# Transposes of 32-bit tiles moved from TensorE to the DMA queue, as two planes of 16 bits

## The chip, the cores and the metric

The kernel runs on one core of a Trainium2 chip. The core has TensorE (PE; PEld is its weight load), VectorE (DVE), ScalarE (ACT), GpSimd (POOL), SyncE (SP), which here only issues DMAs, and 16 DMA engines. The time of a run is device microseconds (us) from start to end; lower is better. A profiled execution has its own time, and inside it a span, which the trace covers.

## What is computed

```python
def reference(A_x, A_wqkv, A_wo, B_x, B_w1, B_w2):     # B_x is not used
    xn = layernorm(A_x)                                  # [1, 2048, 640], eps 1e-5
    q, k, v = split(xn @ A_wqkv)                         # 32 heads of 20
    # each position attends to 8 positions: itself, 2, 4, ... 14 before it
    s = softmax_attention(q, k, v, scale=20 ** -0.5) @ A_wo
    g = silu(silu(xn @ B_w1) @ B_w2)                     # 640 -> 1536 -> 640
    return A_x + s * g
```

All tensors are 32-bit floats. The kernel keeps their precision by splitting both sides of a product into a high part (the number as a float32r) and a low part, the rest. A product is then three matmuls: high x high, low x high, high x low.

## The kernel before

**Tiles and stages.** The 2048 rows are worked on in four groups of 512, that is four token tiles of 128 (T = 4). A group holds every second position of one half of the sequence (`groups`, L193), four of them on each partition, so that positions 2 apart are neighbours. For each group there are two stages. `qkv_phase` (L731) multiplies the transposed input by wqkv in four quarters of the heads (NQ = 4, eight heads each): five units of the inner dimension (DC = 5) for four token tiles, three matmuls each, into four of six PSUM banks (acc). `ffn_phase` (L945) runs the feed-forward: twelve hidden chunks of 128 (FC = 12), each an `up` (L895, 15 matmuls into one of two PSUM banks, rot) and a `down` (L922, 24 matmuls into acc). Its order is a list from `plan` (L288): w1 0, then pairs of two up and two down. `wo_phase` (L798) of the group before, the output projection, stands after w1 0. The last group's projection is `wo_last` (L842), after everything else.

**Attention on DVE.** `evac_qkv` (L526) copies a quarter from PSUM to Q and KV on ACT, `halo` (L539) shifts KV by one and two partitions by four DMAs on SP's queue (L548), `scores` (L565) and `values` (L588) do the attention on DVE with operations of 2560 elements, an exp on ACT between them (L586) from L into E. The result is O, one tile for all of a group's 640 columns. DVE works on a group while TensorE is in its feed-forward stage and in the next group's qkv stage.

**Transposes.** A matmul needs its 128 inner elements on the partitions, so the normalized input (XIN) and O must be turned. The first group's input is turned on TensorE in `first_quarter` (L669). All others go through `split_t` (L503): four transposes of 128x128 on TensorE (L509) into one rot bank, a copy of the high part on ACT (L513) to TH, and the low part on DVE (L519, L516) to TL. One call turns one chunk, 128 of the 640 columns for all four token tiles. The input's five chunks stand between the pairs of the feed-forward stage of the group before, with a second copy on ACT (L515) that frees the rot bank. O's five chunks (`o_chunk`, L615) stand in the next group's qkv stage, after the last units of quarters 1, 2 and 3 (`O_AT`, L769). In the last group three chunks of O stand between single up and down units (`OL_AT`, L192; `SINGLE`, L32), and the last two chunks are turned by halves of the token tiles (`o_rest`, L619), the second half inside the last up. OH and OL, where O's halves go, are the same memory as TH and TL, 16 elements on.

**The order.** The functions only record operations. `Weave` (L65) then places them in time with a cost for each, and the program is written out in that order. TensorE's order is that of recording. On the other engines the earliest ready operation goes first, by priority among those (a priority of 140 or more gives way to others that are ready soon, L136). DMAs on SP have an issue cost, a rate (`RATE`, L75) and a landing time. Each engine then runs its instructions strictly in the written order, and waits where an input is not there. SP's queue carries raw weights, stores of the split weights, loads of x, the halo shifts and the output; POOL's queue the loads of split weights, which each later use reads back from memory. Weights lie in a ring of seven buffers (WR).

Of the kernel before, what the change touches and what calls it, by code (L numbers as in the profile page):

```python
# [8 lines left out]
F32 = mybir.dt.float32  # L9
F32R = mybir.dt.float32r  # L10
AF = mybir.ActivationFunctionType
# [20 lines left out]
SINGLE = 6  # L32
# [32 lines left out]
class Weave:  # L65
# [9 lines left out]
    RATE = 310e3  # L75
# [104 lines left out]
def local_attention_silu_ffn(ctx: ExitStack, tc: tile.TileContext, x, wqkv, wo, w1, w2, out):  # L180
# [11 lines left out]
    OL_AT = {8: 0, 9: 1, 10: 2}  # L192
# [95 lines left out]
    def plan(g):  # L288

        last = g == NG - 1
        todo = [("w1", 0)] + [("wo", 0)] * (g > 0)
        down = 0
        f = 1
        while f < FC:
            k = f // 2
            pair = f + 1 < FC and not (last and f > SINGLE)
            if not last and 1 <= k <= DC:
                todo.append(("x", k - 1))  # L300
            if last and f in OL_AT:
                todo.append(("o", OL_AT[f]))
            if last and f == FC - 1:
                todo.append(("rest", (0, 1)))
# [198 lines left out]
    def split_t(src, skeys, c, i, to, whole=None):  # L503

        ps, kp = rot()

        def turn():
            for t in range(T):
                nc.tensor.transpose(ps[:, tsl(t)], src[:, t, c * P:(c + 1) * P], ident)  # L509
        pe(0.44, turn, skeys, [kp])  # L510
        hi, lo = to[0][i][:, c, :], to[1][i][:, c, :]
        kh, kl = t_keys(i, [c], kinds=["th"]), t_keys(i, [c], kinds=["tl"])
        act(TOK, lambda: nc.scalar.activation(hi, ps, AF.Copy), [kp], kh, 0)  # L513
        if whole is not None:
            act(TOK, lambda: nc.scalar.activation(whole, ps.rearrange("p (t n) -> p t n", n=P), AF.Copy), [kp] + skeys, [("whole", c)], 0)  # L515
            dve(TOK, lambda: nc.vector.tensor_tensor(out=lo.rearrange("p (t n) -> p t n", n=P), in0=whole,  # L516
                in1=hi.bitcast(F32).rearrange("p (t n) -> p t n", n=P), op=OP.subtract), kh + skeys + [("whole", c)], kl, 0, lock=True)
            return
        dve(TOK, lambda: nc.vector.tensor_tensor(out=lo, in0=ps, in1=hi.bitcast(F32), op=OP.subtract),  # L519
            [kp] + kh, kl, 0)  # L520
# [44 lines left out]
    def scores(g, q):  # L565
        i = q % 2
        l, e, m, kv, qq = L[i], E[i], M[i], KV[q], Q[q]
# [18 lines left out]
        act(256, lambda: nc.scalar.activation(e, l, AF.Exp, scale=SCALE), kl, [("e", i)], 0.5, "exp")  # L586

    def values(g, q):  # L588
        i = q % 2
        e, z, kv = E[i], Z[i], KV[q]  # L590
# [3 lines left out]
            out=z[:, 0], in_=e.rearrange("p t w h -> p t h w"), axis=AX.X, op=OP.add), [("e", i)], [("z", i)], pr)  # L594
        dve(200, lambda: nc.vector.reciprocal(out=z[:, 1], in_=z[:, 0]), [], [("z", i)], pr)
        dve(256, lambda: nc.vector.tensor_tensor(out=e, in0=e, in1=win(z[:, 1], W, 0), op=OP.mult),
            [("z", i)], [("e", i)], pr, lock=True)
        for t in range(0, T, 2):
# [7 lines left out]
                in1=v, op=OP.mult), [("e", i)] + hk, PRK, pr, lock=True)  # L606
# [7 lines left out]

    def o_chunk(g, c, i):  # L615
        qs = range(c * P // CQ, ((c + 1) * P - 1) // CQ + 1)
        split_t(O, [("o", q, t) for q in qs for t in (0, 2)], c, i, (OH, OL))

    def o_rest(g, ts, i):  # L619

        ps, kp = rot()
        cs = slice(DC - 2, DC)
        v = ps.rearrange("p (c n) -> p c n", c=2)
        hi, lo = (o[i][:, cs, ts[0] * P:(ts[-1] + 1) * P] for o in (OH, OL))

        def turn():
            for k, c in enumerate(range(DC)[cs]):
                for n, t in enumerate(ts):
                    nc.tensor.transpose(v[:, k, tsl(n)], O[:, t, c * P:(c + 1) * P], ident)  # L629
        pe(0.44, turn, [("o", q, ts[0]) for q in (NQ - 2, NQ - 1)], [kp])  # L630
        kh, kl = (t_keys(i, range(DC)[cs], ts, [k]) for k in ("th", "tl"))
        act(TOK, lambda: nc.scalar.activation(hi, v, AF.Copy), [kp], kh, 0)
        dve(TOK, lambda: nc.vector.tensor_tensor(out=lo, in0=v, in1=hi.bitcast(F32), op=OP.subtract), [kp] + kh, kl, 0)
# [134 lines left out]

    O_AT = {(1, 4): (0, 1), (2, 4): (2, 3), (3, 4): (4,)}  # L769
# [23 lines left out]
    def gkeys(ts, cs):  # L793
        return [("g", t, cs.start) for t in range(ts.start, ts.stop)]
# [47 lines left out]
    def wo_last(g, i):  # L842
# [13 lines left out]
        def give(p, kp, t, cs):  # L856
            n = cs.stop - cs.start
            dve(n, lambda: nc.vector.tensor_tensor(out=G[:, t, cs], in0=p, in1=G[:, t, cs], op=OP.mult),  # L858
                [kp], [("g", t, cs.start)], 0)
            dve(n, lambda: nc.vector.tensor_tensor(out=xr[t][:, cs], in0=xr[t][:, cs], in1=G[:, t, cs], op=OP.add),  # L860
                [("g", t, cs.start)], kx(t, cs)[1:], 0, lock=True)
# [33 lines left out]
    def up(g, i, f, io):  # L895
# [11 lines left out]
        at = 2 if g == NG - 1 and f == FC - 1 else DC  # L907
        for a, b in ((0, at), (at, DC)):
            if a == b:
                continue  # L910
            if a:
                o_rest(g, (2, 3), io)
                wo_rest(g - 1, io)
            pe(3 * (b - a) * mm(TOK), lambda a=a, b=b: first(range(a, b)), t_keys(i, range(DC)) + [kh, kl], [kp])
# [29 lines left out]

    def ffn_phase(g, i, ix, io):  # L945
        if g + 1 < NG:
            load_x(g + 1, 0, 2)
            load_x(g + 1, 2, 2)
            for t in range(T):
                ln_stats(t)  # L950
            ln_rstd(0, T)
            for t in range(T):
                ln_apply(t)
        ps = None
        for kind, f in plan(g):
            if kind == "w1":
                up(g, i, f, io)
            elif kind == "wo":
                wo_phase(g - 1, io)
            elif kind == "x":  # L960
                split_t(XIN, [("xin", t) for t in range(T)], f, ix, (TH, TL), XIN[:, :, tsl(f)])
            elif kind == "o":
                o_chunk(g, f, io)
            elif kind == "rest":
                o_rest(g, f, io)
            else:
                ps = ps or tm_banks()
                down(f, ps)
        for p, kp, ts, cs in tm_views(ps):
            n = (ts.stop - ts.start) * (cs.stop - cs.start)  # L970
            act(n, lambda p=p, ts=ts, cs=cs: nc.scalar.activation(G[:, ts, cs], p, AF.Silu), [kp], gkeys(ts, cs), 0, "silu")
# [40 lines left out]
```

## Time and profile before

| | |
|---|---|
| Median of 3 runs | 636.61 us (636.52 to 636.62) |
| The profiled execution | 636.8 us |
| Its span | 635.0 us |
| TensorE busy | 629.7 us, 99% |
| DVE, ACT, POOL busy | 538.1, 220.6, 112.9 us |
| DMA | 160.82 MB, mean 253 GB/s |

Busy time counts what an engine executes, without waits and without issuing DMAs. A group of the trace is one line of the kernel, engine and operation, with output, inputs, shape and count, then its busy time, the mean of one in ns, and the idle time of the engine before it with what ended it. A matmul's duration is a latency: several are in flight at once. The chain of waits follows the work that ended last back from the end, and its pieces don't overlap.

### The profile page before, as it was taken

The page shows a single profiled execution, that of the slowest core. Times are in us where ns is not written, and L with a number is a line of the kernel's source. Part 1 is how long each engine was busy: PE and PEld are TensorE (multiplying, and loading weights), DVE is VectorE, ACT ScalarE, POOL GpSimd, SP SyncE. Part 2 cuts the span into 40 slices and gives each one's busy share as a digit, 9 for nine tenths or more (in the row PEclk, how much of TensorE's full clock was granted, in tenths as well). Part 3 has the DMA queues.
Part 4 walks back from the last instruction along what each step waited for, and adds up shares of the span by engine and source line. Part 5 has one row for each costly group of instructions (what it writes and reads, how often), then busy time and mean ns, then how long its engine had stood idle before and what let it go on. Part 6 is the DMA issues. An engine that isn't in the chain of part 4 may idle for free.

```text
span 635.0 us, 9113 instructions
## 1 busy us (share of the span) xinstructions
PE 629.7 (99%) x3503; PEld 570.1 (90%) x3503; DVE 538.1 (85%) x548; ACT 220.6 (35%) x459; POOL 112.9 (18%) x159
## 2 busy tenths in 40 slices
PE   9999999999999999999999999999999999999997
PEld 7888899998889999999888999999988999999997
DVE  6599899999999969998969998999605999999734
ACT  5436455443436024242423512323313232223230
POOL 4500000001110161111221115311222211111100
PEclk9999999999999999999999999999999999999999
DMA  9999999768997997567798998856779998666552
GB/s 294 310 304 318 319 395 375 311 220 245 297 311 221 283 292 247 175 191 211 204 255 208 310 361 305 287 176 183 220 197 268 247 324 251 182 191 195 189 177 83
DMA packets 77500, 160.82 MB, mean 253 GB/s; under 512 B 9248, under 2 KB 38912, under 8 KB 77456
## 3 DMA queue, kind: packets, MB, share of 16 engines
q0 software_dynamic: 25952, 79.31, 42.7%
q1 hardware_dynamic: 50960, 80.52, 39.7%
q8 instruction: 27, 0.44, 0.3%
q10 hardware_dynamic: 544, 0.41, 0.2%
q14 instruction: 17, 0.14, 0.1%
HBM read 107.91 MB, written 34.16 MB: 224 GB/s over the span
## 4 chain that ended last, share of the span: by engine, by line
PE 99%; DVE 0%; POOL 0%; issue 0%; POOLq 0%
PE acc L780 22%; PE acc L782 15%; PE acc L748 10%; PE acc L749 10%; PE acc L747 10%; PE rot L904 9%; PE rot L906 9%; PE rot L905 9%; PE rot L509 2%; PE acc L690 2%; PE rot L642 1%; PE rot L669 0%; PE rot L890 0%; PE rot L629 0%; DVE gate L858 0%; DVE xin L860 0%
## 5 line engine op out<-in xcount | busy, mean ns | idle before, releaser
L571 DVE TENSOR_TENSOR pr<-q,kv 128x2560 f32<-128x2560 f32 x32 | 90.3, 2820 | 34.0 <-DMA kv<-kv 33.8
L747 PE MATMUL acc<-w,th 128*128 128x512 f32 (+2 forms) x300 | 113.3, 378 | 0.0
L780 PE MATMUL acc<-w,sh 128*128 128x384 f32 x384 | 113.2, 334 | 0.0
L749 PE MATMUL acc<-w,th 128*128 128x512 f32 (+2 forms) x300 | 112.9, 376 | 0.0
L748 PE MATMUL acc<-w,tl 128*128 128x512 f32 (+2 forms) x300 | 112.9, 376 | 0.0
L782 PE MATMUL acc<-w,sh 128*128 128x256 f32 x384 | 107.1, 279 | 0.0
L904 PE MATMUL rot<-th,w 128*128 128x512 f32 x240 | 95.8, 399 | 0.0
L906 PE MATMUL rot<-th,w 128*128 128x512 f32 x240 | 93.8, 391 | 0.0
L905 PE MATMUL rot<-tl,w 128*128 128x512 f32 x240 | 93.6, 390 | 0.0
L603 DVE TENSOR_TENSOR pr<-e,kv 128x2560 f32<-128x2560 f32 x32 | 90.3, 2823 | 0.7
L574 DVE TENSOR_REDUCE l<-pr 128x128 f32<-128x2560 f32 x32 | 90.1, 2815 | 0.4
L437 POOL DMA_DIRECT2D w<-half_q x52 | 37.4, 719 | 237.8 <-PE rot L906 115.1
L437 POOL DMA_DIRECT2D w<-half_w x72 | 38.6, 536 | 215.6 <-PE acc L782 87.5
L608 DVE TENSOR_TENSOR pr<-pr 128x1280 f32<-128x1280 f32 x64 | 73.8, 1153 | 1.0
L782 PEld LDWEIGHTS acc<-w,sh 128*128 128x128 f32 x384 | 72.2, 188 | 1.0
L780 PEld LDWEIGHTS acc<-w,sh 128*128 128x128 f32 x384 | 72.1, 188 | 1.0
L917 ACT ACTIVATE sh<-rot 128x512 fp32r<-128x512 f32 x48 | 28.8, 600 | 125.4 <-PE rot L906 125.4
L749 PEld LDWEIGHTS acc<-w,th 128*128 128x128 f32 x300 | 56.3, 188 | 8.7
L748 PEld LDWEIGHTS acc<-w,tl 128*128 128x128 f32 x300 | 56.3, 188 | 8.6
L747 PEld LDWEIGHTS acc<-w,th 128*128 128x128 f32 x300 | 56.3, 188 | 8.5
L780 PE MATMUL acc<-w,sl 128*128 128x384 f32 x192 | 57.8, 332 | 0.0
L906 PEld LDWEIGHTS rot<-th,w 128*128 128x128 f32 x240 | 45.0, 188 | 9.9
(96 smaller groups left out, 993.1 us busy)
## 6 DMA issues: line engine op xcount, KB each, us to landing
w<-half_w POOLq DMA_DIRECT2D x72, 640.0 KB, 4.9
w<-half_q POOLq DMA_DIRECT2D x39, 512.0 KB, 4.6
half_w<-w SPq DMA_DIRECT2D x24, 640.0 KB
kv<-kv SPq DMA_DIRECT2D x16, 560.0 KB
kv<-kv SPq DMA_DIRECT2D x16, 420.0 KB
w<-half_wo POOLq DMA_DIRECT2D x10, 640.0 KB, 5.3
gate<-in_B_w_dram SPq DMA_DIRECT2D x16, 320.0 KB
w<-half_q POOLq DMA_DIRECT2D x13, 384.0 KB, 5.0
```

The lines of the kernel that those rows point to most:

```text
L437: add("POOL", 1.0, lambda: nc.gpsimd.dma_start(both, src), [("half", u), ("half", u, "more")], [kh, kl], due + 10, nbytes=2 * n * P * 4)
L571: dve(2560, lambda t=t: nc.vector.tensor_tensor(out=PR, in0=win(qq[:, t:t + 2, :], W, 0), in1=win(kv[:, 0, t:t + 2, :], W, CQ), op=OP.mult ...
L574: dve(2560, lambda t=t: nc.vector.tensor_reduce(out=l[:, t:t + 2].rearrange("p t w h -> p (t w h)"), in_=PR.rearrange("p t w (h d) -> p (t ...
L603: dve(2560, lambda t=t, v=v: nc.vector.tensor_tensor(out=PR.rearrange("p t w (h d) -> p t (w h) d", d=DH), in0=e[:, t:t + 2].rearrange("p ...
L747: nc.tensor.matmul(o, hi, wh, start=c == 0, stop=False)
L748: nc.tensor.matmul(o, lo, wh, start=False, stop=False)
L749: nc.tensor.matmul(o, hi, wl, start=False, stop=c == DC - 1)
L780: nc.tensor.matmul(a[t][0][:, :CA], st, w[:, :CA], start=first, stop=last)
L782: nc.tensor.matmul(b[t // 2][0][:, h * CB:(h + 1) * CB], st, w[:, CA:], start=first and h == 0, stop=last, skip_group_check=True)
L904: nc.tensor.matmul(h, wh[:, cs], TH[i][:, c, :], start=c == 0, stop=False)
L905: nc.tensor.matmul(h, wh[:, cs], TL[i][:, c, :], start=False, stop=False)
L906: nc.tensor.matmul(h, wl[:, cs], TH[i][:, c, :], start=False, stop=c == DC - 1)
```

## The change

`split_t`, `o_chunk` and `o_rest` go, and with them every transpose on TensorE past the first group's input. In their place stand `turn_chunk`, `turn_o` and `turn_rest`. A new scratch tile, `TURN`, has 512 words of 32 bits for each partition. For one chunk, ACT copies the chunk as 1024 16-bit numbers into TURN, the low halves of all words ahead of the high halves (two planes). Two DMA transposes on SP's queue, one for each plane, write the planes back, turned, in the chunk's own place in XIN or O. ACT copies them into TURN again, as words. From TURN, ACT makes the high part and DVE the low part. All chunks use the one tile, so one chunk follows the other.

- The input's chunks are recorded right behind wo in the feed-forward stage (behind w1 0 in the first group), and O's chunks at the end of that stage; both have priority 150. In the last group three chunks of O and two passes of `turn_rest` follow wo.
- `plan` has pairs throughout, also in the last group, and wo stands after the first pair (after w1 0, 1, 2) and no longer after w1 0. The last up is no longer cut in two.
- To make room for TURN, E becomes the last 64 of the 160 columns of each token tile of Q, of the same quarter, and the last group's gate lies in KV[0] (`GL`).
- The planner's `RATE` goes from 310e3 to 380e3.

```diff
-    RATE = 310e3
+    RATE = 380e3
...
-    E = tiles("e", 2, [P, T, W, HQ])
+    E = [v[:, :, CQ - W * HQ:].rearrange("p t (w h) -> p t w h", w=W) for v in Q]
...
+    GL = KV[0].rearrange("p s t m -> p (s t m)")[:, :T * D].rearrange("p (t d) -> p t d", t=T)
...
+    TURN = sb.tile([P, TOK], F32, name="turn")
...
-        todo = [("w1", 0)] + [("wo", 0)] * (g > 0)
+        todo = [("w1", 0)]
...
-            pair = f + 1 < FC and not (last and f > SINGLE)
+            pair = f + 1 < FC
...
+            if f == 1 and g:
+                todo.append(("wo", 0))
...
+    def halves_of(v, hi, lo, kh, kl):
+        act(TOK, lambda: nc.scalar.activation(hi, v, AF.Copy), ["turn"], kh, 0)
+        dve(TOK, lambda: nc.vector.tensor_tensor(out=lo, in0=v, in1=hi.bitcast(F32), op=OP.subtract),
+            ["turn"] + kh, kl, 0, lock=True)
...
+    def turn_chunk(src, keys, c, i, to, prio):
+
+        place = src[:, :, c * P:(c + 1) * P].bitcast(U16)
+        flat = place.rearrange("p t (h n) -> p h t n", h=2)
+        planes = TURN.bitcast(U16).rearrange("p (h n) -> p h n", h=2)
+        act(2 * TOK, lambda: nc.scalar.activation(
+            planes.rearrange("p h (t n) -> p h t n", t=T), place.rearrange("p t (n h) -> p h t n", h=2), AF.Copy),
+            keys, ["turn"], prio)
+        for h in range(2):
+            dma(lambda h=h: nc.sync.dma_start_transpose(flat[:, h], planes[:, h]), ["turn"], [("plane", h)],
+                P * TOK * 4, clock[0], 0.65)
+        act(2 * TOK, lambda: nc.scalar.activation(
+            TURN.bitcast(U16).rearrange("p (t n h) -> p h t n", t=T, h=2), flat, AF.Copy),
+            [("plane", 0), ("plane", 1)] + keys, ["turn"], prio)
+        halves_of(TURN, to[0][i][:, c, :], to[1][i][:, c, :], t_keys(i, [c], kinds=["th"]), t_keys(i, [c], kinds=["tl"]))
+
+    def turn_rest(ts, i):
+
+        cs = slice(DC - 2, DC)
+        keys = [("o", q, ts[0]) for q in (NQ - 2, NQ - 1)]
+        bits = TURN.bitcast(U16).rearrange("p (t c h n) -> p t c h n", t=2, c=2, h=2)
+        whole = TURN.rearrange("p (c n) -> p c n", c=2)
+        for k, t in enumerate(ts):
+            place = O[:, t, cs.start * P:].bitcast(U16)
+            act(4 * P, lambda k=k, place=place: nc.scalar.activation(
+                bits[:, k], place.rearrange("p (c n h) -> p c h n", c=2, h=2), AF.Copy), keys, ["turn", ("turn", k)], 0)
+            dma(lambda k=k, place=place: nc.sync.dma_start_transpose(
+                place.rearrange("p (b n) -> p b n", n=P), bits[:, k].rearrange("p c h n -> p (c h n)")),
+                [("turn", k)], [("plane", k)], P * TOK * 4, clock[0], 0.65)
...
-                    if g and (q, c) in O_AT:
-                        for k in O_AT[q, c]:
-                            o_chunk(g - 1, k, io)
...
+    def turn_ahead(g, ix, io):
+
+        if g < NG - 1:
+            for c in range(DC):
+                turn_chunk(XIN, [("xin", t) for t in range(T)], c, ix, (TH, TL), 150)
+            return
+        for c in range(DC - 2):
+            turn_o(g, c, io)
+        for ts in ((0, 1), (2, 3)):
+            turn_rest(ts, io)
+        wo_rest(g - 1, io)
...
+            if kind == ("wo" if g else "w1") and f == 0:
+                turn_ahead(g, ix, io)
+        if g < NG - 1:
+            for c in range(DC):
+                turn_o(g, c, i)
```

More of the change, by code (lines that the diff above doesn't have):

```diff
@@ L10 @@
 F32R = mybir.dt.float32r
+U16 = mybir.dt.uint16
 AF = mybir.ActivationFunctionType
@@ L31 @@
 NS = 3
-SINGLE = 6
 RAW_AHEAD = 10
@@ L523, in q_keys, with turn_o @@
+    def turn_o(g, c, i, prio=150):
+        qs = range(c * P // CQ, ((c + 1) * P - 1) // CQ + 1)
+        turn_chunk(O, [("o", q, t) for q in qs for t in (0, 2)], c, i, (OH, OL), prio)
     def q_keys(q, t):
@@ L613, in values @@
                 PRK, [("o", q, t)], pr, lock=True)
[L615 to L633, printed above, removed]
     def first_quarter(i):
@@ L791, in tm_views, with gkeys @@
             yield b[k][0].rearrange("p (t m) -> p t m", t=2), b[k][1], slice(2 * k, 2 * k + 2), slice(CA, D)
-    def gkeys(ts, cs):
-        return [("g", t, cs.start) for t in range(ts.start, ts.stop)]
+    def gkeys(ts, cs, name="g"):
+        return [(name, t, cs.start) for t in range(ts.start, ts.stop)]
     TM = mm(CA) + mm(CB)
@@ L906, in first @@
                 nc.tensor.matmul(h, wl[:, cs], TH[i][:, c, :], start=False, stop=c == DC - 1)
[L907 to L914, printed above, removed]
+        pe(3 * DC * mm(TOK), lambda: first(range(DC)), t_keys(i, range(DC)) + [kh, kl], [kp])
         w_done()
@@ L959, in ffn_phase @@
                 wo_phase(g - 1, io)
[L960 to L965, printed above, removed]
             else:
```

61 lines of the change are left out of this document (24 added, 37 removed).

## The prediction, made before the result

> **What bounds the kernel now.** I read the page first, then PE's waits, the chain of waits, the windows, and last the groups of the lines that the diff touches.
>
> ```profile
> span 635.0 us, 9113 instructions
> ...
> PE 629.7 (99%) x3503; PEld 570.1 (90%) x3503; DVE 538.1 (85%) x548; ACT 220.6 (35%) x459; POOL 112.9 (18%) x159
> ...
> PEclk9999999999999999999999999999999999999999
> DMA  9999999768997997567798998856779998666552
> ...
> PE 99%; DVE 0%; POOL 0%; issue 0%; POOLq 0%
> ```
>
> ```profile
> PE rot L642 <- POOL ident masks.py:199: 1.4, 1, 1.4
> ```
>
> TensorE is busy for 99% of the span at full granted clock, the chain that ended last is 99% TensorE, and in the view of waits its only listed wait is 1.4 us at the start. So whatever leaves TensorE's stream shortens the span one for one, until something else makes TensorE wait. Two other rows say where such a wait could come from: DMA is busy for half of its time or more in all slices but the last, and DVE is nearly full in the first group's feed-forward stage (columns of the windows view: PE, PEld, DVE, ACT and POOL busy, clock, DMA share, GB/s):
>
> ```profile
> 80.00:152.00 72.00, 72.00 (x415) 65.65 (x414) 70.75 (x76) 35.32 (x58) 3.75 (x5) 1.00 0.87 317
> ```
>
> ACT has 35.3 of 72 us there. ACT is the engine that the change loads.
>
> **What leaves TensorE.** The groups of the removed transposes, then their place in the chain:
>
> ```profile
> L509 PE MATMUL rot<-ident,o 128*128 128x128 f32 x72 | 9.8, 272 | 0.0
> ...
> L509 PE MATMUL rot<-ident,xin 128*128 128x128 f32 x60 | 9.0, 272 | 0.0
> ...
> L629 PE MATMUL rot<-ident,o 128*128 128x128 f32 x8 | 1.3, 279 | 0.0
> ```
>
> ```profile
> 79.84 0.44 PE rot L509 x4
> ...
> 602.51 0.43 PE rot L629 x4
> 604.36 0.66 PE rot L629 x4
> 626.87 2.60 PE acc L780 x15
> 629.47 1.72 PE rot L890 x15
> ```
>
> 132 transposes at L509 are 33 chunks of four: 15 of the normalized input and 18 of the attention output. The mean of 272 ns is a latency; the transposes overlap, and four of them hold the chain for 0.44 us (all 33 chunks are in the chain, at 0.43 to 0.44 us each; the eights show 0.87). 33 x 0.436 = 14.4 us. The two L629 pieces are 0.43 + 0.66 = 1.1 us, the second with a short wait in it. **Removed: 15.5 us.** The matmuls of up, down and wo keep their number: the last group's up units only go in pairs, and wo goes two up units later with its products, additions and stores, which nothing on TensorE waits for.
>
> The Trainium skill, "TensorE: Matmul & The Clock Gate", Part 4: PE-mode transpose, gives about 275 ns for a 128x128 transpose in a kernel. The trace agrees on the duration (272) but not on its worth: by the page 140 x 0.275 = 38.5 us would go and the time would be about 598; the chain gives 0.11 us each.
>
> **What is added.** Each chunk now goes through one scratch tile (turn): an ACT copy of 1024 16-bit elements into two planes, two DMA transposes of 128 KB on SP's queue, an ACT copy of 1024 elements back, ACT's hi copy, DVE's lo. The last four half-chunks (turn_rest) go in two passes of two and two copies of 512. That is 35 passes and 70 DMAs. Rows for ACT and DVE:
>
> ```profile
> L917 ACT ACTIVATE sh<-rot 128x512 fp32r<-128x512 f32 x48 | 28.8, 600 | 125.4 <-PE rot L906 125.4
> L918 ACT ACTIVATE sf<-rot 128x512 f32<-128x512 f32 x48 | 28.5, 593 | 4.6 <-DVE sl L919 4.6
> ...
> L586 ACT ACT_TABLE_LOAD x14 | 18.0, 1283 | 0.2
> ...
> L446 ACT ACTIVATE w<-xr 128x640 fp32r<-128x640 f32 x18 | 13.1, 758 | 7.8 <-PE acc L748 2.4 <-issue 2.0 <-PE acc L782 1.7
> ...
> L515 ACT ACTIVATE xin<-rot 128x512 f32<-128x512 f32 x15 | 8.9, 592 | 0.0
> ...
> L586 ACT ACTIVATE e<-l 128x256 f32<-128x256 f32 x16 | 6.7, 420 | 43.4 <-DVE l L584 43.3
> ```
>
> ```profile
> L516 DVE TENSOR_TENSOR tl<-xin,th 128x512 fp32r<-128x512 f32 x15 | 10.3, 688 | 6.9 <-ACT xin L515 6.9
> ```
>
> - *ACT.* No row has 1024 16-bit elements. By bytes such a copy is the 128x512 one, 0.60 us; by elements it is two of those, 1.2 us. 420 ns at 256 and 758 ns at 640 elements is 0.88 ns an element, so 1.1 us; I take 1.1. ACT gets 33 x 2.2 + 8 x 0.6 = 77 us, loses the 15 xin copies (8.9), and by the built order has four more table loads (35 against 31, 5.1 us): 220.6 becomes some 294 us, 47% of the new span. Off the path, as long as no waiting ACT instruction keeps others back.
> - *DVE.* lo is 0.69 us as before. E now lies in Q's columns, so Q is held until values has read it; KV of the same quarter is held by the same reads already. The tightest place is the last quarter of the first group:
>
> ```profile
> 184.25 0.49 DVE L611 TENSOR_TENSOR o<-pr 128x320 f32<-128x320 f32 x1
> ```
>
> ```profile
> 198.89 0.44 ACT L530 ACTIVATE kv<-acc 128x320 f32<-128x320 f32 x1 [4.11 <-PE acc L749]
> ```
>
>   14 us lie between the last read and the next write; TensorE comes at most 10 x 0.44 us sooner. Nothing.
> - *DMA and SP.* 70 x 128 KB is 9.2 MB on 160.8 MB. At the page's mean of 253 GB/s that is 36 us of transfer spread over the run. An SP issue (L548) has a median of 0.87 us, so a pair takes 1.7 us of SP, and the ten in the first group take 9 us of SP's queue, in which the raw weights stand:
>
> ```profile
> L548 SPq DMA_DIRECT2D kv<-kv x64: 614/870/2242, 25.1 to 514.9; - x64
> ```
>
> ```profile
> ACT w L446 <- PE acc L748: 15.5, 7, 4.0
> ```
>
>   The weight splits wait mostly for TensorE to give up a buffer of the ring of seven, so the weights are there some six units ahead (a unit is 2.6 us or more): about 16 us of cover for 9. Nothing.
>
> **The new wait, T.** The copy back waits for both transposes. Call T the time from the end of the first copy until both planes have landed. ACT runs in order: behind the copy back stand the evacuations of rot and acc that TensorE needs. No row has a DMA transpose. From below, the first load of the kernel (160 KB, issue to use); from above, the kv shifts, SBUF to SBUF on the same queue, 1.1 MB in four DMAs:
>
> ```profile
> 0.75 0.39 SPq L700 DMA_DIRECT2D xin<-in_A_x_dram  x1
> ```
>
> ```profile
> 3.81 0.89 DVE L655 BATCH_NORM_STATS2 st<-xin 128x6 f32<-128x320 f32 x2 [2.36 <-DMA xin<-in_A_x_dram]
> ```
>
> ```profile
> 472.36 4.53 SPq L548 DMA_DIRECT2D kv<-kv  x4
> ```
>
> ```profile
> 484.04 2.83 DVE L571 TENSOR_TENSOR pr<-q,kv 128x2560 f32<-128x2560 f32 x1 [27.68 <-DMA kv<-kv]
> ```
>
> ```profile
> w<-half_w POOLq DMA_DIRECT2D x72, 640.0 KB, 4.9
> w<-half_q POOLq DMA_DIRECT2D x39, 512.0 KB, 4.6
> ```
>
> 3.1 us below; 11.7 us above. A pair of 256 KB is nearer to the small load: one more issue of 0.87 before it and one for itself, 3.06 + 1.74 = **4.8 us**, which is also what the larger weight loads take. That is an estimate.
>
> How much T is covered? Feed-forward comes in pairs: two up, two down.
>
> ```profile
> 80.28 0.23 PE rot L904
> ...
> 87.13 0.18 PE acc L780
> ...
> 94.02 0.44 PE rot L509 x4
> ```
>
> A pair is 94.02 - 80.28 = 13.7 us. In it ACT has two evacuations (2 x 1.19), one pass (2 x 1.1 + 0.6), and about half an exp with two table loads (0.5 x 3.0): 6.7 us. 7.0 remain, less the 0.7 us of lo, for which the next pass waits: 6.3. Beyond that sh may be late once by the 6.85 us of the two units that run before it is used. So a group with four passes in its pairs loses 4 x (T - 6.3) - 6.85 us, if that is positive. In the qkv stages the built order puts one pass in a quarter, nearly always with the first copy before the eight to twelve evacuations of a quarter and the copy back after them: cover of some 10 us. In wo (120 matmuls, 17 us) two passes stand, with no evacuation needed. O's fifth chunk is needed in its last fifth: 1.1 + 4.8 + 1.1 + 0.6 + 0.7 = 8.3 us of 13.7.
>
> At T = 4.8 the loss is nothing. DVE's order can still hold a lo, and behind it the next pass, for one of its 2.8 us operations; I put half of one, 1.4 us, on the path once.
>
> **The end.** The last attention output comes here:
>
> ```profile
> 591.90 0.49 DVE L611 TENSOR_TENSOR o<-pr 128x320 f32<-128x320 f32 x1
> ...
> 599.25 0.49 DVE L611 TENSOR_TENSOR o<-pr 128x320 f32<-128x320 f32 x1
> ```
>
> wo's last token tile starts at 626.87, the third 2.60 + 1.72 = 4.3 us earlier, at 622.6, the first at 613.9. In the last group ten chunks go, so these come 4.4 us sooner against DVE: 618.2 and 609.5. A rest pass is 4 x 0.6 + 4.8 + 0.6 + 0.7 = 8.5 us: the first is done at 592.4 + 8.5 = 600.9, the second at 609.4. Both in time; at T = 10 the second would be late by 2 us.
>
> **Sum.** The profiled run took 636.8 us, 1.8 outside its span; the median of the three is 0.2 below. 636.8 - 15.5 + 1.4 = **622.7 us**.
>
> **Rivals.**
> 1. *Part of it is eaten.* T is 8.5 to 9.2. With T = 9, 3 x (4 x (9 - 6.3) - 6.85) = 11.9 us come back: 621.3 + 11.9 = 633. For it: DMA at 0.87 and more in the first group, and a queue that runs in order, so a pair behind four kv shifts waits for them. Against: in the pairs of later groups hardly anything else stands in SP's queue. DVE as the bound of the first group (98% busy) would cost less, the 2.2 us of its five chunks.
> 2. *ACT is held, and the kernel is slower.* The mechanism: the copy back stands in ACT's queue for T, sh behind it, TensorE behind sh. It decides from 4 x (T - 6.3) - 6.85 = 15.5 / 3, which is T = 9.3. If a pair takes what the four kv shifts took, 11.7 us, three groups lose 3 x 14.75 = 44 us: 666. For it: that row is the only SBUF-to-SBUF one, and 16-bit elements may go slower than long rows. Against: its bytes are four times as many. The Trainium skill, "VectorE: DVE Perf Modes", The three transpose paths, speaks for this rival: it has 390 ns on TensorE and 1309 ns by DMA for a 128x128 block of 16 bits, and advises TensorE where PSUM will do. Eight such blocks in a row would be an estimate of 10.5 us and a time of about 651. No row here can show that figure; whether the blocks overlap decides.
> 3. *More is gained*, if a transpose costs TensorE more than its place in the chain: 599 by its 272 ns latency (140 x 0.272 = 38 us). The chain speaks against it.
>
> That the transposes don't go at all is excluded: the built order has none past the first group's 20.
>
> **Chances.** A difference under 0.2% (1.3 us) can't be told from none. Forecast (up to 627) 0.56; rival 1 (627 to 635) 0.14; within 0.2% 0.04; rival 2 0.24, of which 0.17 above 642; rival 3 0.02. Faster 0.72, same 0.04, slower 0.24. The forecast's own range is 620.5 to 627. For 8 in 10: 620.5 (all 15.5 gone and nothing added gives 621.1 by the median) to 642.
>
> **What would show it.** TensorE with 3363 matmuls, without L509 and about 614 us busy; its waits still near nothing; ACT near 294 us; the planes landing some 5 us after the first copy; 16-bit copies at 1.1 us. Wrong would be: TensorE idle in front of L904 or L747 behind an ACT evacuation, with ACT idle on the two planes; copies far over 1.2 us; raw weights late in the first group.

## The result, and the profile after

The changed kernel takes 691.4 us (median of four executions, 681.5 to 696.2) against 636.6 (636.5 to 636.6) for the kernel before on the same chip. The ratio of 1.078, with a 95% interval of 1.066 to 1.090, is that of the two faster executions (681.5 and 690.4 us); the profiled one is one of the two slower, at the same granted clock (0.965, the others 0.957 to 0.966). The forecast of 622.7 and its range up to 642 are missed on the side of rival 2.

The page of the changed kernel, profiled in an execution of 692.4 us, answers line for line to that of before:

```profile
span 690.6 us, 9047 instructions
...
PE 635.0 (92%) x3363; PEld 567.9 (82%) x3363; DVE 544.5 (79%) x548; ACT 298.8 (43%) x522; POOL 110.9 (16%) x159
...
PEclk9999899999999999998999897999999799999999
DMA  9899999996999899994899897988499899466862
...
PE 35%; DMA 25%; DVE 16%; ACT 12%; SPq 7%; issue 5%; POOL 0%; ACTq 0%; DVEq 0%
DMA o<-turn 9%; PE acc L780 8%; DMA xin<-turn 8%; PE acc L782 6%; PE acc L752 3%; PE acc L753 3%; PE acc L754 3%; SPq L513 3%; PE rot L904 3%; PE rot L905 3%; PE rot L906 3%; ACT turn L515 3%; DVE l L599 3%; ACT turn L509 2%; DVE pr L628 2%
```

TensorE has the 3363 matmuls that were forecast, and yet 5.3 us more busy time. It no longer makes the chain: 35% of it is TensorE, and 17% is the landing of transposes (o<-turn and xin<-turn). The span grew by 55.6 us: 15.5 went with the transposes; TensorE's idle time went from 5.3 to 55.6 us (+50.3); and the matmuls that are left took 635.0 in place of 629.7 - 15.5 = 614.2 us (+20.8). The three add up: -15.5 + 50.3 + 20.8 = 55.6.

TensorE's waits, and below them ScalarE's on the scratch tile (total us, times, longest us):

```profile
PE rot L904 <- ACT sf L911: 14.3, 4, 6.7
PE acc L752 <- ACT q L561: 9.7, 2, 9.3
PE acc L780 <- DVE sl L912: 8.3, 4, 2.7
PE acc L780 <- DVE gate L812: 7.6, 2, 5.1
```

```profile
ACT turn L515 <- DMA o<-turn: 62.4, 13, 9.9
ACT turn L515 <- DMA xin<-turn: 60.5, 13, 12.3
ACT turn L515 <- DVE o L636: 24.9, 4, 7.5
```

ScalarE stands still for 147.8 us in front of the copy back (L515), and TensorE waits for what is behind that copy in ScalarE's queue: evacuations of a quarter, silu's second copy, and through VectorE its lo. One wait of the list is of another kind: the longest for silu's second copy (6.7 us, at 80.2) stands in number 2 below too (6.4 us, at 77.1), where nothing is transferred.

VectorE is held as well, in front of the chunk's own lo (L499), and TensorE behind it for the gate: 71.7 us of VectorE in all. Its group, and then one case in the timelines of ScalarE, VectorE and TensorE:

```profile
L499 DVE TENSOR_TENSOR tl<-turn,th 128x512 fp32r<-128x512 f32 x35 | 26.5, 758 | 71.7 <-ACT th L498 71.7
```

```profile
409.18 1.36 ACT L515 ACTIVATE turn<-xin 128x1024 uint16<-128x1024 uint16 x1 [12.29 <-DMA xin<-turn]
```

```profile
411.24 0.69 DVE L499 TENSOR_TENSOR tl<-turn,th 128x512 fp32r<-128x512 f32 x1 [7.23 <-ACT th L498]
```

```profile
418.10 0.69 PE L780 MATMUL acc<-w,sh 128*128 128x384 f32 x1 [5.12 <-DVE gate L812]
```

Behind the lo of 411.24 stand 5.6 us of attention work on VectorE, and behind that, at 417.5, the product with the gate that frees TensorE's accumulator.

A wait behind an evacuation, from end to end, in the timelines of ScalarE, SP and TensorE (start us, length us, what; in brackets the idle time before it and what ended it):

```profile
536.15 1.06 ACT L509 ACTIVATE turn<-o 128x1024 uint16<-128x1024 uint16 x1 [3.85 <-DVE tl L499]
...
540.06 0.42 ACT L611 ACTIVATE q<-l 128x256 f32<-128x256 f32 x1 [1.54 <-DVE l L609]
546.59 1.34 ACT L515 ACTIVATE turn<-o 128x1024 uint16<-128x1024 uint16 x1 [6.12 <-DMA o<-turn]
547.96 0.63 ACT L498 ACTIVATE th<-turn 128x512 fp32r<-128x512 f32 x1
548.50 0.42 ACT L555 ACTIVATE kv<-acc 128x320 f32<-128x320 f32 x1
```

```profile
537.24 2.53 SPq L513 DMA_TRANSPOSE o<-turn  x2
```

```profile
549.25 0.69 PE L752 MATMUL acc<-w,th 128*128 128x384 f32 x1 [9.26 <-ACT q L561]
549.74 0.52 PE L753 MATMUL acc<-w,tl 128*128 128x384 f32 x1
550.06 0.52 PE L754 MATMUL acc<-w,th 128*128 128x384 f32 x1
...
555.11 0.34 PE L752 MATMUL acc<-w,th 128*128 128x384 f32 x1
555.29 0.34 PE L753 MATMUL acc<-w,tl 128*128 128x384 f32 x1
```

The first copy ends at 537.2, both transposes are issued at once with nothing ahead of them in SP's queue, and the planes are there some 9.3 us later. Nothing else runs on ScalarE for 6.1 us, the evacuations (kv, q) wait behind the copy back, and TensorE has no free accumulator for 9.26 us. Then comes a second price: the matmuls of 384 columns start 0.32 us apart until 555, and 0.17 to 0.18 apart from there on. The windows show the granted clock (last column but two):

```profile
549.00:552.00 3.00, 2.75 (x9) 2.75 (x10) 3.00 (x2) 2.04 (x11) 0.16 (x1) 0.50 0.00 0
552.00:555.00 3.00, 3.00 (x11) 3.00 (x10) 2.93 (x3) 0.00 (x0) 0.37 (x1) 0.50 0.98 228
555.00:558.00 3.00, 3.00 (x19) 3.00 (x18) 2.97 (x2) 0.00 (x0) 0.88 (x2) 1.00 0.89 243
```

Over the span the granted clock is 0.965, and 614.2 / 0.965 = 636.5 us, close to the 635.0. So the 20.8 us are, as far as a mean can say it, the same matmuls at half clock behind waits; the mean counts idle time too, and only the wait above was followed. The Trainium skill, "TensorE: Matmul & The Clock Gate", Part 1, says that an idle array falls to half clock and gets full clock back only after some 3.4 us of work. The trace agrees with the half; here it lasted 5.7 us.

### The profile page after: what moved, and what is told of

The parts are those of the page before. It is cut to its first block, busy times and chain, and to the rows that moved or that the text cites. A ratio compares the mean times of both kernels' runs of the same rounds, so it can differ in the third digit from the quotient of the medians.

```text
span 690.6 us, 9047 instructions
## 1 busy us (share of the span) xinstructions
PE 635.0 (92%) x3363; PEld 567.9 (82%) x3363; DVE 544.5 (79%) x548; ACT 298.8 (43%) x522; POOL 110.9 (16%) x159
## 4 chain that ended last, share of the span: by engine, by line
PE 35%; DMA 25%; DVE 16%; ACT 12%; SPq 7%; issue 5%; POOL 0%; ACTq 0%; DVEq 0%
DMA o<-turn 9%; PE acc L780 8%; DMA xin<-turn 8%; PE acc L782 6%; PE acc L752 3%; PE acc L753 3%; PE acc L754 3%; SPq L513 3%; PE rot L904 3%; PE rot L905 3%; PE rot L906 3%; ACT turn L515 3%; DVE l L599 3%; ACT turn L509 2%; DVE pr L628 2%
## 5 line engine op out<-in xcount | busy, mean ns | idle before, releaser
L780 PE MATMUL acc<-w,sh 128*128 128x384 f32 x384 | 118.5, 345 | 10.0 <-DVE gate L812 7.6
L782 PE MATMUL acc<-w,sh 128*128 128x256 f32 x384 | 110.3, 287 | 1.9 <-DVE gate L812 1.8
L904 PE MATMUL rot<-th,w 128*128 128x512 f32 x240 | 96.3, 401 | 14.3 <-ACT sf L911 14.3
L905 PE MATMUL rot<-tl,w 128*128 128x512 f32 x240 | 95.8, 399 | 0.0
L906 PE MATMUL rot<-th,w 128*128 128x512 f32 x240 | 95.6, 398 | 0.0
L596 DVE TENSOR_TENSOR pr<-q,kv 128x2560 f32<-128x2560 f32 x32 | 90.2, 2820 | 5.3 <-DMA kv<-kv 4.9
L628 DVE TENSOR_TENSOR pr<-q,kv 128x2560 f32<-128x2560 f32 x32 | 90.3, 2823 | 0.8
L780 PEld LDWEIGHTS acc<-w,sh 128*128 128x128 f32 x384 | 74.9, 195 | 12.1 <-DVE gate L812 8.2
L499 DVE TENSOR_TENSOR tl<-turn,th 128x512 fp32r<-128x512 f32 x35 | 26.5, 758 | 71.7 <-ACT th L498 71.7
L782 PEld LDWEIGHTS acc<-w,sh 128*128 128x128 f32 x384 | 75.1, 196 | 3.9 <-DVE gate L812 3.1
L752 PEld LDWEIGHTS acc<-w,th 128*128 128x128 f32 x300 | 57.2, 191 | 22.5 <-ACT q L561 10.3
L780 PE MATMUL acc<-w,sl 128*128 128x384 f32 x192 | 59.8, 342 | 8.5 <-DVE sl L912 8.3
L754 PEld LDWEIGHTS acc<-w,th 128*128 128x128 f32 x300 | 57.2, 191 | 8.7
```

Source lines behind the costliest of these rows:

```text
L596: dve(2560, lambda t=t: nc.vector.tensor_tensor(out=PR, in0=win(qq[:, t:t + 2, :], W, 0), in1=win(kv[:, 0, t:t + 2, :], W, CQ), op=OP.mult ...
L628: dve(2560, lambda t=t, v=v: nc.vector.tensor_tensor(out=PR.rearrange("p t w (h d) -> p t (w h) d", d=DH), in0=e[:, t:t + 2].rearrange("p ...
L752: nc.tensor.matmul(o, hi, wh, start=c == 0, stop=False)
L754: nc.tensor.matmul(o, hi, wl, start=False, stop=c == DC - 1)
L780: nc.tensor.matmul(a[t][0][:, :CA], st, w[:, :CA], start=first, stop=last)
L782: nc.tensor.matmul(b[t // 2][0][:, h * CB:(h + 1) * CB], st, w[:, CA:], start=first and h == 0, stop=last, skip_group_check=True)
```

## The experiments

Each was run once beside the kernel before (636.3 to 636.8 us) and profiled, except where several runs are named. A caution holds for all: any change of a price in the planner rewrites the order on all engines but TensorE. Only the second and third kernel keep the changed kernel's written order. And kernels that wait scatter: the four executions of the changed kernel span 14.7 us, so a difference of single runs of a few us says little.

**1. The rest of the change without DMA transposes.** The kernel before with the change's other edits, but for two: the last up stays cut in two, for the transposes within it, and the last group's gate stays where it was.

```
-    RATE = 310e3
+    RATE = 380e3
-    OL_AT = {8: 0, 9: 1, 10: 2}
+    OL_AT = {5: 0, 7: 1, 9: 2}
-    E = tiles("e", 2, [P, T, W, HQ])
+    E = [v[:, :, CQ - W * HQ:]... for v in Q]
 (pairs to the last group's end, wo after w1's first pair)
```

> The kernel before with the rest of the change and no DMA transposes: rate 380e3 in the planner, pairs throughout, wo two up units later, E in Q. The transposes stay on TensorE. If the loss comes from the new passes through ACT and DMA: 636 to 640 us. If the new order of the units or the planner's rate costs TensorE time by itself: 650 us or more.

Measured: 648.0 us, between the two ranges. I had expected no change or little; these edits cost 11 us by themselves.

**2. The changed kernel's order without the transfers.** 

```
-            dma(lambda h=h: nc.sync.dma_start_transpose(flat[:, h], planes[:, h]), ["turn"], ...
+            dma(lambda: None, ["turn"], ...
```

> The changed kernel in the same written order, with the 70 transposing DMAs left out; the copy back takes the words where they lie, so the data is not turned. ACT keeps both copies of each pass. If the wait for the planes is the cause (ACT stands at the copy back): 621 to 626 us, TensorE without waits and at full clock. If the 77 us of copies on ACT, or DVE's order behind them, are the cause: 660 us or more.

Measured: 634.8 us, 9 over the range for the wait and far under the other. All copies of ScalarE are there (299.8 us busy), TensorE is busy for 617.8 us at a clock of 0.995, and one large wait is left:

```profile
PE 617.8 (98%) x3363; PEld 556.1 (88%) x3363; DVE 545.5 (86%) x548; ACT 299.8 (47%) x522; POOL 111.4 (18%) x159
```

```profile
PE rot L903 <- ACT sf L910: 6.4, 1, 6.4
```

The transfers and the waits for them are 691.4 - 634.8 = 56.6 us (47 to 61 over the changed kernel's four executions). The rest of the change, ScalarE's copies among it, costs 634.8 - 621.1 (before less 15.5) = 13.7. Number 1 has 11.4 us without any such copy, so little is left for the copies; no run has them alone.

**3. Plain copies of the same bytes.** 

```
-            ... nc.sync.dma_start_transpose(flat[:, h], planes[:, h]) ...
+            ... nc.sync.dma_start(flat[:, h], planes[:, h].rearrange("p (t n) -> p t n", n=P)) ...
```

> The changed kernel in the same written order, with 70 plain DMAs of the same 128 KB in place of the transposing ones; the data is not turned. If any DMA of this size is late in SP's queue beside the other traffic: 680 to 700 us, as with the transposes. If the transpose itself is the slow part (its issue of 1.26 us, its landing): 622 to 640 us.

Measured: 668.8 us, between the two ranges. O's transfers on SP in the changed kernel, then in this one (ns min/median/max of an issue; then us to landing):

```profile
L513 SPq DMA_TRANSPOSE o<-turn x36: 1189/1259/3415, 128.0 to 640.7; - x36
...
DMA to landing us min/median/max: 3.4/8.6/15.2
```

```profile
L513 SPq DMA_DIRECT2D o<-turn x36: 594/640/980, 127.5 to 617.7; - x36
...
DMA to landing us min/median/max: 3.4/5.0/13.0
```

So 34.0 of the 56.6 us come with any transfer in that place of the queue, and 22.6 (13 to 27 over the four executions) because it transposes: twice the issue, a landing 3.6 us later in the median.

**4. An honest price.** The planner is told 1.26 us of issue and 4.5 us more to land, so that it puts ScalarE's other work between the two copies:

```
-                P * TOK * 4, clock[0], 0.65)
+                P * TOK * 4, clock[0], 1.26, 4.5)
```

> The changed kernel with nothing but the planner's price of a transpose changed: 1.26 us to issue (0.65 before) and 4.5 us more to land, so that it writes the copies back behind other work of ACT. If ACT standing at the copy back holds TensorE: 630 to 650 us, with less ACT idle time on the planes. If the single scratch tile's chain of passes or the DMA traffic itself is the bound: 670 us or more, with waits moved elsewhere.

Measured: 660.1 us, again between the two ranges. ScalarE's waits for the planes fall from 122.9 to 48.2 us. What TensorE waits for now:

```profile
PE rot L905 <- ACT sf L912: 8.2, 1, 8.2
PE acc L781 <- ACT th L499: 7.0, 2, 3.7
PE acc L781 <- DVE tl L500: 6.7, 2, 6.1
```

L781 serves down and wo; where it waits for th or tl it is wo, and these four waits lie at 542 to 559 us, in the wo of the last group's feed-forward stage: O's last chunks of the group before come too late for it.

**5. The same with the rate of before.**

```
-    RATE = 380e3
+    RATE = 310e3
```

> The whole change with the honest price of a transpose, and RATE 310e3 in place of 380e3 (660.1 us). By the 7.3 us that the rate alone was worth without transposes (648.0 against 640.6), 650 to 655 us: the gap of 8.2 us at 79 us goes, O's late chunks at 542 to 559 us (13 us of gaps) stay. If the two gains do not add (with fewer loads early the transposes of x get in earlier and O's come late in another place), 656 to 662 us.

Measured: 730.8 us, 69 over the wider of the two ranges. wo waits in all three groups for th and tl:

```profile
PE acc L781 <- ACT th L499: 40.9, 6, 9.4
PE acc L781 <- DVE tl L500: 21.1, 6, 6.5
```

With slower loads in its model the planner starts O's chunks later: the last of the first group at 246.0 us, where number 4 had it at 217.0. An honest price is therefore no cure for the whole change: one number of the model moves it by 70 us.

**6 and 7. Two scratch tiles**, odd chunks through the gate's or XIN's first 2 KB, at RATE 380e3 and 310e3. These two kernels do not compute what the reference does, for a reason that is open, and only their times are used.

```
+        if c % 2:
+            tile, kt = (G[:, 0, :TOK], [...]) if src is XIN else (XIN[:, 0, :TOK], [...])
```

> The run with the honest price of a transpose (660.1 us), with one thing more: every second chunk goes through a second 2 KB tile (the gate's while x is turned, XIN's while O is turned), so that a chunk need not wait until the one ahead of it has left the tile. If the chain through the one tile made O's last chunks late there (TensorE's gaps at 542 to 559 us, 13 us in all, and ScalarE's 53 us before the first copy for the lo of the chunk ahead), those gaps go and the time is 642 to 650 us; the 8.2 us gap at 79 us stays. If the transfers themselves are what is late, whatever the tile, both stay and the time is 655 to 662 us. Slower than 662 if the second tile's loads and gates now wait for passes.

> The same two tiles and the honest price, with the planner's RATE of the kernel before (310e3) in place of 380e3. If the planner's faster rate makes the stall in group 1 (a split of weights on ScalarE that the written order puts ahead of a silu and whose load is late: 6.4 us without transposes, 8.2 us with the price), that stall goes and the time is 6 to 10 us under the run with two tiles at 380e3. If the transposes' own traffic makes it, the two are within 3 us. Below 636.6 us only if both theories hold and the clock goes up with the waits.

Measured: 694.0 and 668.8 us. The first is the case of waits for a second tile (over 662), the second is 25 us under the first and so outside both of its ranges. Against 660.1 and 730.8 with one tile that is worse once and better once. They settle nothing on the tile.

**8. x alone by DMA**: the kernel before, x's 15 chunks by DMA at the honest price, E in Q's columns, RATE 310e3, O on TensorE.

```
+            if kind == ("wo" if g else "w1") and f == 0 and g < NG - 1:
+                for c in range(DC):
+                    turn_chunk(XIN, ..., c, ix, (TH, TL), 150)
```

> The kernel before with only x's 15 chunks by DMA (E in Q's columns, one tile, honest price, RATE 310e3, O's chunks, the places of wo and the single chunks of the last group as before): TensorE loses 15 x 0.436 = 6.5 us. If the loss sits in O's passes (the transposes held on SP by the values' write of O, and ScalarE's copy back in front of q and th that TensorE needs at once), this is 630 to 637 us. If any pass in the SP queue costs, x's as well as O's, it is 640 to 650 us.

Measured: 630.9 us, in the first range and faster than before.

**9. Number 1 with the rate of before** (the one-line edit of number 5).

> The rest of the change without any transpose by DMA (648.0 us with RATE 380e3), with RATE 310e3: if the rate makes its 11 us, 637 to 639 us; if the pairs to the end, wo after the first pair and E in Q's columns make them, 645 to 649 us.

Measured: 640.6 us, between the two. The rate makes 7.3 of the first experiment's 11.4 us; 4.2 stay with the other edits.

**10. O alone by DMA**, at the honest price and RATE 310e3, x on TensorE. Against number 8:

```
-                    turn_chunk(XIN, ..., c, ix, (TH, TL), 150)
+        if g < NG - 1:
+            for c in range(DC):
+                turn_o(g, c, i)
 (the last group's chunks by turn_ahead, as the change has them; x as before)
```

> The mirror of the run with only x turned by DMA (630.9 us, 5.5 under the kernel before): only O's chunks by DMA (15 of the first three groups, 3 and two pairs of pieces of the last), x's by TensorE as before, the honest price, RATE 310e3, wo and the single chunks of the last group where the kernel before has them. TensorE loses 20 x 0.436 = 8.7 us less 2.2 that the last pieces took. If O's passes carry the loss, TensorE waits for them and the time is 640 to 655 us. If the loss came of the number of passes in all (35 through one tile), and 15 to 20 passes fit, it is 628 to 634 us.

Measured: 701.1 us, 46 over the range for a loss by O. At this price the loss is O's. The last chunk of the first group, in the timelines of SP, VectorE, ScalarE and TensorE, and the windows beside it (the last three columns are the granted clock, the DMA share and GB/s):

```profile
210.28 5.14 SPq L518 DMA_TRANSPOSE o<-turn  x2
...
228.85 0.49 DVE L660 TENSOR_TENSOR o<-pr 128x320 f32<-128x320 f32 x1 [6.00 <-DMA o<-turn]
229.42 1.34 ACT L520 ACTIVATE turn<-o 128x1024 uint16<-128x1024 uint16 x1 [19.17 <-DVE o L660]
...
231.48 0.69 PE L826 MATMUL acc<-w,th 128*128 128x384 f32 x1 [14.92 <-ACT th L503]
```

```profile
216.00:222.00 6.00, 0.56 (x4) 0.30 (x3) 5.91 (x3) 0.00 (x0) 0.53 (x1) 0.78 1.44 140
222.00:229.00 7.00, 0.00 (x0) 0.00 (x0) 0.98 (x2) 0.00 (x0) 0.00 (x0) 0.50 1.03 160
```

The two transposes leave SP by 215.4 and are there by 228.8, with the DMA engines fully busy (a share of 1.44 and 1.03) at 140 to 160 GB/s; TensorE stands in wo. ScalarE's 19.2 us are put down to VectorE's write, but that write had itself waited for the planes, and took 0.5: the planes decided. That VectorE's write waits for the planes at all, though it fills other columns of O, I put down to a tie of regions: a chunk's columns are one strided region of O. Number 16 shows that the tie goes when the planes land elsewhere; the reason for it is argued.

**11. O lands elsewhere**, in XIN, at the honest price and RATE 310e3 (the fifth kernel, one move).

```
+        if src is O:
+            flat, land = XIN[:, 0, :TOK].bitcast(U16).rearrange("p (h t n) -> p h t n", h=2, t=T), [("xin", 0)]
```

> The whole change with the honest price and RATE 310e3, with one thing more: O's transposes land in the first 2 KB of XIN, free once x is turned, in place of O's own columns, so that neither the transposes wait for the values' write of other columns of O nor that write for the transposes (after: 67.3 us of SP's queue and 15.7 us of VectorE). If this tie makes O's passes late, the time is 5 us or more under that of the same kernel without the move (e5_told_310). If the tie is beside the path, the two are within 3 us.

Measured: 812.8 us, 82 slower still, which neither range allowed. Without the tie wo waits for 146 us on th and tl; x's loads now wait for O's passes as well.

**12 and 13. x alone and O alone at the change's own price.**

```
-                P * TOK * 4, clock[0], 1.26, 4.5)
+                P * TOK * 4, clock[0], 0.65)
```

> Only x's 15 chunks by DMA at RATE 310e3, as in the run of 630.9 us, but with the price that the change itself gives a transpose (0.65 us of issue, no landing of its own). If the written order with a price far too low is what loses time, copies back now stand ahead of silu and evacuations and the time is 637 to 655 us. If x's passes are harmless because nothing needs them before the group's end, 629 to 633 us.

> Only O's chunks by DMA at RATE 310e3, as in the run of 701.1 us, but at the change's own price (0.65 us). If the price decides and the honest one only pushed O's chunks behind everything, 640 to 665 us. If O's chunks fail by their place (one tile, last quarter's values, wo at once after), 690 us or more at this price too.

Measured: 638.6 and 664.1 us. For x the price is worth some 7 us (638.6 against 630.9, and 631.8 in number 15), and at the low one x alone is no gain but 2.3 us slower than the kernel before (636.3): ScalarE waits before the copy back, by the view of its waits,

```profile
ACT turn L522 <- DMA xin<-turn: 52.4, 8, 19.7
```

and once TensorE with it (4.4 us at L804, behind sh). For O the low price is the better one by 37 us. One reason is in the traces: O's last chunk then comes before wo in the second group (its copy back at 363.2 us, wo at 376.6) and not after it (410.1 and 375.8). Both lose against the kernel before.

**14. x, and O's first two chunks of three groups.** Against number 8:

```
-    O_AT = {(1, 4): (0, 1), (2, 4): (2, 3), (3, 4): (4,)}
+    O_AT = {(2, 4): (2, 3), (3, 4): (4,)}
...
+        if g < NG - 1:
+            for c in range(2):
+                turn_o(g, c, i)
```

> The run of 630.9 us (x by DMA at the honest price) with the first two chunks of O of the first three groups by DMA as well: TensorE loses 6 x 0.436 = 2.6 us more. If O's chunks cost by their deadline, these two, whose quarters are ready 30 to 60 us before wo, are free: 628 to 631 us. If any transpose into O's columns holds the values' write and ScalarE's copy back, 635 us or more.

Measured: 646.6 us: six chunks more cost 15.7 us in place of saving 2.6. The one tile is now taken from 34 to 483 us with one long break, at 343 to 373 (21 passes, 21.2 us from one to the next in the median). TensorE stands idle for 18.5 us, 11.8 more than in number 8. The longest of its waits is the tie of number 10 again, in the timelines of VectorE and TensorE:

```profile
462.74 0.49 DVE L639 TENSOR_TENSOR o<-pr 128x320 f32<-128x320 f32 x1 [6.23 <-DMA o<-turn]
463.15 0.68 DVE L947 TENSOR_TENSOR sl<-sf,sh 128x512 fp32r<-128x512 f32 x1
```

```profile
463.89 0.69 PE L808 MATMUL acc<-w,sl 128*128 128x384 f32 x1 [5.11 <-DVE sl L947]
```

ScalarE had written sf by 455.9; VectorE's lo of it (sl) stood behind the write of O, and that behind the planes.

**15. x alone again, timed.** 

> The run with only x's 15 chunks by DMA, priced honestly, RATE 310e3, again and timed: 630 to 632 us, 0.7 to 1.0% under the kernel before. If the first time was a stroke of luck of the queues, 633 us or more.

Measured: 631.8 us (631.2 to 633.8, five runs) against 636.4: a ratio of 0.992, interval 0.991 to 0.994. The page of the slowest of the five, and who waited for the transposes:

```profile
span 632.0 us, 9048 instructions
...
PE 622.8 (99%) x3443; PEld 561.9 (89%) x3443; DVE 539.7 (85%) x548; ACT 249.8 (40%) x476; POOL 111.3 (18%) x159
...
PEclk9999999999999999999999999999999999999999
```

```profile
ACT turn L522: 13.2, 4
```

TensorE lost 6.9 us of busy time for 15 x 0.436 = 6.5 forecast, and kept the full clock. From the end of the first copy to the copy back it is now 14.6 us in the median: the planner has put ScalarE's other work between them, and ScalarE waits for the planes 13.2 us in all, against 52.4 in number 12.

**16. The changed kernel, O landing in XIN** (the edit of 11; price and rate as the change has them).

> The changed kernel as it is (its price, RATE 380e3) with one move: O's chunks land in the first 2 KB of XIN in place of O's own columns, so that no transpose waits for the values' write of O and no such write or copy back for a transpose (in the changed kernel 67.3, 15.7 and 24.9 us of SP's, VectorE's and ScalarE's waits). If this tie is a main part of the 55 us, 655 to 675 us. If the waits for the transfers as such and the one tile make the loss, 685 us or more.

Measured: 674.4 us. In the changed kernel SP's queue, loads and all, stood behind that tie, and so did VectorE:

```profile
SPq L513 <- DVE o L636: 67.3, 4, 27.3
```

```profile
DVE o L636 <- DMA o<-turn: 15.7, 4, 6.6
```

Both are gone, and 17 us with them (7 to 22 over the changed kernel's four executions), as the first range had it; since the order changes too, that is a size and no proof. ScalarE's waits for planes stay:

```profile
ACT turn L518 <- DMA xin<-turn: 110.5, 26, 14.6
```

**17. Number 14 with O landing in XIN.**

> x and O's first two chunks of three groups by DMA (646.6 us), with O's landing in XIN's first 2 KB, so that nothing ties them to the values' write. If the tie costs the 16 us, 628 to 633 us. If the one tile and the queue cost them, 640 us or more.

Measured: 647.5 us, no gain. The tie is gone and with it the wait of 5.1 us, but TensorE now waits 10.9 us for th and tl of turned chunks, 6.8 of them in wo. So the tie is not all of number 14's 16 us; how much it is, this run can't say, since landing in XIN also ties O's passes to the loads of x.

## Why the prediction was wrong, point by point

- *What bounds the kernel, what leaves TensorE.* Right. In number 2 TensorE's 617.8 us at 0.995 are 614.7 at full clock, for "about 614"; x alone gave back 6.9 us for 60 transposes. Rival 3 (0.272 us each, 16.3) is out.
- *ACT.* Right: the first copy took 1.06 us for 1.1, the copy back 1.37 (over my upper bound of 1.2), ScalarE 298.8 for 294.
- *The step that failed is "At T = 4.8 the loss is nothing".* Both sides of it were wrong, the wait T and the cover of 6.3 us a pass. I took T from an unloaded load with an issue of 0.87. An issue took 1.26, two make 2.5 us, and from the end of the first copy to the copy back the 33 whole chunks of the changed kernel took 4.0 us at best, 8.4 in the median, 9.3 in the mean, 16.8 at most, some of it ScalarE's own work; 15 of them were over the 9.3 from which rival 2 was to decide.
- *The cover, under "How much T is covered?", is the larger part.* By my formula the mean of 9.3 us gives back just 15.5 us, and the time would have been about 637; number 2 against the changed kernel shows 56.6. The other 41 are what the formula left out. It spread waits evenly over pairs. It had no evacuation of a quarter behind a copy back (9.26 us in one place), no VectorE held for the lo (71.7 us, 5.1 of them passed on to TensorE in one place), no tie through O's columns, and no half clock after a wait (TensorE is busy for 635.0 us in place of number 2's 617.8 with the same matmuls). How the 41 divide among these is not shown. Rival 2 had the sign and the start of it: ScalarE held at the copy back, sh behind it, TensorE behind that.
- *The written order.* It was planned with a transpose of 0.65 us to issue and no more time to land than any other DMA. I read that order as built and took its cover from it; but a low price only puts ScalarE's next work right behind a copy back that has to wait.
- *The rest of the change.* The sum has no term for the rate, and holds that nothing on TensorE waits for wo in its new place. Number 1 has 11.4 us there, 7.3 of them by RATE.
- *The end.* Right: both rest passes were in time, TensorE's last long wait is 1.3 us.
- *Rival 2's prices.* 666 by the kv shifts, and 651 by the Trainium skill's 1309 ns a block ("VectorE: DVE Perf Modes", The three transpose paths), were both under 691.4. The page's figure times eight blocks, 10.5 us, is not T either: a pair was through in 4.0 us at best, so the time of one block does not add up over eight. What makes the median 8.4 is not taken apart here.

The 68.7 us by which the sum is short are the 56.6 of the transfers and the 13.7 that number 2 shows without them, less 1.4 that the sum had allowed and 0.2 between the profiled run and the median.

What is shown: with the order kept, the transfers make the loss, 56.6 us, 34.0 with any transfer there and 22.6 as transposes, within the scatter given above. x's transposes alone gain at the honest price (0.992 of the time) and lose 2.3 us at the low one, in one run; O's alone lose at both. For x the price alone decides between gain and loss, and the waits of ScalarE for the planes go with it.

What is only argued: why O fails where x goes free. x is needed at the group's end, O at wo. The count of passes through the one tile may be a part of it: a group is some 153 us, and the changed kernel's ten passes at its 16.9 us are 169, which do not fit; but number 14's seven at its 21.2 are 149, which do. Whether the one tile, the tie or the order holds number 14 is open, and so is the share of each in the whole change.

## What to carry to other kernels

A transfer on the way of an engine that serves others is priced by what waits behind it in that engine's queue, not by its length: take its time from loaded rows, and ask which other work the order puts behind it. Give the planner the measured price, but measure again: it helped x by 7 us and cost O 37. Move the part with slack (x: 0.992 of the time) and leave the part that the next stage waits for (O). Look for ties between a landing transfer and writers of other columns of the same tile; taking one away is a trial and no rule, for it gave 17 us here in one kernel, none in a second, and cost 82 in a third.

## What the runs showed of the hardware

- A TensorE wait can be paid twice. After 9.26 us without work the granted clock was 0.50 for 5.7 us. Over whole spans: 1.000 in number 15, 0.965 in the changed kernel, 0.893 with the 812.8 us.
- A transpose of 128 KB by DMA holds SP's queue for 1.26 us, a plain copy of as many bytes for 0.64; in the same written order O's landed after 8.6 and 5.0 us in the median. The Trainium skill, "Advanced Engine Details and Errata", X-Bar Transpose, has transposing DMAs as fast as others; here that holds for the shortest landing alone (3.4 us in both).
- ScalarE's two 16-bit copies of 1024 elements differ: 1.06 us where it takes words apart into planes, 1.37 where it puts planes together again into words.
